# A decode kernel on one core: new row shapes for three weight loads, and a new order of loads and products

## Chip, cores, metric

One core of a Trainium2 chip. The metric is device time in microseconds (us), the median of several executions. The granted TensorE clock is 1.00. A run more than 1.5% above the fastest of its kernel counts as slow. Ratios are the mean time of one kernel's fast runs over the mean of the other's of the same rounds, so they are not quite the ratios of the medians quoted beside them.

## The reference

One token goes through two branches that share its input x (576 numbers) and are mixed by a gate:

```python
g = sigmoid((x * gate_w).sum(-1))
q = (x @ wq)                       # 576 x 4096: 32 query heads of 128
k, v = last 4096 positions of 16 K/V heads (two query heads share one)
a = softmax(q k^T / sqrt(128)) v   # per head
a = a @ wo                         # 4096 x 576
b = gelu(x @ w1 + b1) @ w2 + b2    # 576 x 4608, 4608 x 576
return g * a + (1 - g) * b
```

Everything is bf16. Little is computed and much is read, 53.6 MB in all: K and V are 16 loads of 1 MiB each, wq 4.7 MB, w1, w2 5.3 MB each, wo 4.7 MB.

## The kernel before

All large loads are issued from the SP queue. Most products have one or two moving columns, with the weights as the stationary operand, so that each product on TensorE (PE) needs a weight load of its own (1758 of each in the trace). The first FFN product is the one with w1, the second the one with w2. The parts that matter:

```python
wq_pool = ...tile_pool(name="wq_pool", bufs=3)
for k in range(KT):                      # KT = 5: four tiles of 128 rows, one of 64
    kp = P if k < KFULL else LASTK       # 128, or 64
    wq_k = wq_pool.tile([P, Hq * Dh], BF16, ...)
    nc.sync.dma_start(out=wq_k[:kp, :], in_=A_wq[k*P : k*P+kp, :])
kv_pool = ...tile_pool(name="kv_pool", bufs=5, ...)     # K and V share five buffers
...                                      # x, gate product, q products
for hh in range(5): k_head(hh)           # load K head, 32 products, two exp
w1_t = w1_pool.tile([P, KT, F], BF16)    # five loads, the last of 64 rows
w2_t = w2_pool.tile([P, NF, D], BF16)
nc.sync.dma_start(out=w2_t[:], in_=B_w2.rearrange("(c p) n -> p c n", p=P))   # 1152 B rows
for c in range(NF):                      # first FFN product, 36 chunks
    for k in range(KT):                  # 128, 128, 128, 128, 64 rows
        matmul(ht_ps[:, c:c+1], lhsT=w1_t[:kp, k, c*P:(c+1)*P], rhs=xt[:kp, k:k+1])
    matmul(ht_ps[:, c:c+1], lhsT=b1_row[0:1, ...], rhs=one11)                 # 1 row
...                                      # gelu on DVE and ACT
for hh in range(5, Hkv): k_head(hh)
for c in range(NF):                      # second FFN product
    for j in range(NJ): matmul(acc[j][:, 0:1], lhsT=w2_t[:, c, ...], rhs=gt[:, c:c+1])
    matmul(row[0:1, 512:576], lhsT=gt[:, c:c+1], rhs=w2_t[:, c, 512:576])
...                                      # load wo; per V head: load, 32 products,
                                         # scale, output projection of the head before
```

The text gives no order across engines: the framework schedules this kernel. In the trace K heads 0 to 4 come first, then both FFN products, and K head 5 only after most of the second one.

The softmax here doesn't subtract the row's maximum and nothing guards it: scores larger than these inputs give would overflow.

## Time and profile before

| | before |
|---|---|
| median of the first three runs | 157.19 us (156.29 to 159.23) |
| median of 15 runs | 157.94 us (156.29 to 160.1); of the 12 fast ones 157.64 |
| span of the profiled run | 154.3 us |
| PE busy | 78.8 us, 51% |
| DMA, mean rate | 349 GB/s |

"Span" is one execution in the profile; the measured time is some 2 us more. The prediction below shows the activity rows, the rates by stretch and the waits. One more reading: the stretch of the trace where the second hole ends. Columns are start, duration, engine, line, operation, count.

```profile
74.03 0.99 PE L158 MATMUL s_ps<-qt,kv_t 128*128 128x2 bf16 x32
75.05 7.96 SPq L152 DMA_DIRECT2D kv_t<-in_A_k_cache_dram  x6
```

K head 5's products end at 75.02, and the issue of the next K loads follows at once: the loads had waited for a buffer.

### The profile page before, as it was taken

The page shows a single profiled execution, that of the slowest core. Times are in us where ns is not written, and L with a number is a line of the kernel's source. Part 1 is how long each engine was busy: PE and PEld are TensorE (multiplying, and loading weights), DVE is VectorE, ACT ScalarE, POOL GpSimd, SP SyncE. Part 2 cuts the span into 40 slices and gives each one's busy share as a digit, 9 for nine tenths or more (in the row PEclk, how much of TensorE's full clock was granted, in tenths as well). Part 3 has the DMA queues.
Part 4 walks back from the last instruction along what each step waited for, and adds up shares of the span by engine and source line. Part 5 has one row for each costly group of instructions (what it writes and reads, how often), then busy time and mean ns, then how long its engine had stood idle before and what let it go on. Part 6 is the DMA issues. An engine that isn't in the chain of part 4 may idle for free.

```text
span 154.3 us, 3784 instructions
## 1 busy us (share of the span) xinstructions
PE 78.8 (51%) x1758; PEld 67.8 (44%) x1758; DVE 9.2 (6%) x48; ACT 9.2 (6%) x67; POOL 2.8 (2%) x10
## 2 busy tenths in 40 slices
PE   0181245230007999399996225100266676767671
PEld 0071234220006988377896224100256565656560
DVE  0040000000000000400000000100000000000002
ACT  3000011210000000000123121100000000000000
POOL 7000000000000000000000000000000000000000
DMA  4979999999999999996289999999999999999910
GB/s 146 430 263 357 280 429 418 408 432 423 344 217 356 356 356 400 416 427 255 55 265 397 414 427 361 356 356 390 414 423 416 416 416 418 414 420 414 408 64 2
DMA packets 14802, 53.87 MB, mean 349 GB/s; under 512 B 817, under 2 KB 9538, under 8 KB 9538
## 3 DMA queue, kind: packets, MB, share of 16 engines
q1 hardware_dynamic: 14658, 53.61, 91.5%
q8 instruction: 14, 0.23, 0.6%
q0 software_dynamic: 128, 0.01, 0.1%
q14 instruction: 2, 0.02, 0.0%
HBM read 53.62 MB, written 0.00 MB: 347 GB/s over the span
## 4 chain that ended last, share of the span: by engine, by line
DMA 67%; PE 26%; DVE 2%; issue 1%; SPq 1%; POOL 0%; ACT 0%; DVEq 0%; POOLq 0%
DMA kv_t<-in_A_v_cache_dram 39%; DMA w_t<-in_B_w_dram 15%; DMA kv_t<-in_A_k_cache_dram 9%; PE ht_ps L189 7%; PE acc L238 5%; DMA gw_row<-in_gate_w_dram 4%; PE s_ps L158 3%; PE row L245 3%; PE o_ps L310 3%; PE ht_ps L196 3%; PE qk_ps L133 1%; DVE junk_row L102 0%; DVE out_row L339 0%; POOL x_row L56 0%; PE g_ps L113 0%
## 5 line engine op out<-in xcount | busy, mean ns | idle before, releaser
L310 PE MATMUL o_ps<-et_all,kv_t 128*128 128x2 bf16 x512 | 16.2, 166 | 21.2 <-DMA kv_t<-in_A_v_cache_dram 21.2
L310 PEld LDWEIGHTS <-kv_t 128*128 128x128 bf16 x512 | 14.9, 104 | 23.3 <-DMA kv_t<-in_A_v_cache_dram 23.3
L158 PE MATMUL s_ps<-qt,kv_t 128*128 128x2 bf16 x512 | 15.6, 165 | 16.5 <-DMA kv_t<-in_A_k_cache_dram 16.5
L158 PEld LDWEIGHTS <-kv_t 128*128 128x128 bf16 x512 | 14.6, 104 | 17.4 <-DMA kv_t<-in_A_k_cache_dram 17.3
L189 PE MATMUL ht_ps<-xt,w_t 128*128 128x1 bf16 (+1 forms) x180 | 14.3, 173 | 13.8 <-DMA w_t<-in_B_w_dram 13.8
L189 PEld LDWEIGHTS <-w_t 128*128 128x128 bf16 (+1 forms) x180 | 10.5, 106 | 15.2 <-DMA w_t<-in_B_w_dram 14.2
L238 PE MATMUL acc<-gt,w_t 128*128 128x1 bf16 x144 | 9.6, 170 | 2.4 <-DVE gt L227 2.4
L287 PE MATMUL acc<-ot,wo_t 128*128 128x1 bf16 x128 | 8.2, 167 | 4.0 <-DVE ot L317 4.0
L287 PEld LDWEIGHTS <-wo_t 128*128 128x128 bf16 x128 | 7.1, 105 | 6.0 <-issue 5.0
L166 ACT ACTIVATE et_all<-s_ps 128x32 bf16<-128x32 f32 x32 | 6.2, 204 | 49.8 <-PE s_ps L158 49.8
L238 PEld LDWEIGHTS <-w_t 128*128 128x128 bf16 x144 | 6.7, 106 | 4.6 <-issue 2.3
L133 PE MATMUL qk_ps<-xt,wq_k 128*128 128x1 bf16 (+1 forms) x160 | 4.9, 165 | 6.0 <-DMA wq_k<-in_A_wq_dram 6.0
L245 PE MATMUL row<-w_t,gt 128*1 128x64 bf16 x36 | 7.7, 213 | 0.0
L133 PEld LDWEIGHTS <-wq_k 128*128 128x128 bf16 (+1 forms) x160 | 4.6, 104 | 6.2 <-DMA wq_k<-in_A_wq_dram 6.1
L294 PE MATMUL row<-wo_t,ot 128*1 128x64 bf16 x32 | 6.8, 213 | 0.0
L196 PE MATMUL ht_ps<-one,b_row 1*128 1x1 bf16 x36 | 6.5, 180 | 0.0
L166 ACT ACTIVATION_READ_ACCUMULATOR et_all<-s_ps 128x1 f32 x32 | 6.0, 198 | 0.0
L317 DVE TENSOR_TENSOR ot<-o_ps,rg 128x2 bf16<-128x2 f32 x16 | 2.5, 159 | 49.0 <-PE o_ps L310 49.0
L89 PE MATMUL xt_ps<-one,x_row 1*128 1x1 bf16 (+1 forms) x5 | 0.4, 175 | 6.6 <-DMA x_row<-in_A_x_dram 6.6
L196 PEld LDWEIGHTS <-b_row 1*128 1x128 bf16 x36 | 3.5, 98 | 0.5
L89 PEld LDWEIGHTS <-x_row 1*128 1x128 bf16 (+1 forms) x5 | 0.3, 108 | 6.6 <-DMA x_row<-in_A_x_dram 6.6
L245 PEld LDWEIGHTS <-gt 128*1 128x1 bf16 x36 | 2.8, 79 | 0.5
(50 smaller groups left out, 18.0 us busy)
## 6 DMA issues: line engine op xcount, KB each, us to landing
kv_t<-in_A_k_cache_dram SPq DMA_DIRECT2D x16, 1024.0 KB, 11.7
kv_t<-in_A_v_cache_dram SPq DMA_DIRECT2D x16, 1024.0 KB, 11.4
w_t<-in_B_w_dram SPq DMA_DIRECT2D x1, 5184.0 KB, 35.7
w_t<-in_B_w_dram SPq DMA_DIRECT2D x4, 1152.0 KB, 21.6
wo_t<-in_A_wo_dram SPq DMA_DIRECT2D x1, 4608.0 KB, 25.5
wq_k<-in_A_wq_dram SPq DMA_DIRECT2D x4, 1024.0 KB, 6.1
w_t<-in_B_w_dram SPq DMA_DIRECT2D x1, 576.0 KB, 23.7
wq_k<-in_A_wq_dram SPq DMA_DIRECT2D x1, 512.0 KB
```

Of the source, the lines that this page charges most:

```text
L89: nc.tensor.matmul(xt_ps[:kp, k : k + 1], lhsT=x_row[0:1, k * P : k * P + kp], rhs=one11[0:1, 0:1], start=True, stop=True,)
L133: nc.tensor.matmul(qk_ps[:, j : j + 1], lhsT=wq_k[:kp, j * Dh : (j + 1) * Dh], rhs=xt[:kp, k : k + 1], start=True, stop=True,)
L158: nc.tensor.matmul(s_ps[:, c, :], lhsT=k_t[:, c, :], rhs=qt[:, 2 * hh : 2 * hh + 2], start=True, stop=True,)
L166: nc.scalar.activation(out=et_all[:, hh, :, hq], in_=s_ps[:, :, hq], func=ACT.Exp, scale=SCALE, accum_out=psums[:, 2 * hh + hq : 2 * hh + ...
L189: nc.tensor.matmul(ht_ps[:, c : c + 1], lhsT=w1_t[:kp, k, c * P : (c + 1) * P], rhs=xt[:kp, k : k + 1], start=(k == 0), stop=False,)
L196: nc.tensor.matmul(ht_ps[:, c : c + 1], lhsT=b1_row[0:1, c * P : (c + 1) * P], rhs=one11[0:1, 0:1], start=False, stop=True,)
L238: nc.tensor.matmul(acc[j][:, 0:1], lhsT=w2_t[:, c, j * P : (j + 1) * P], rhs=gt[:, c : c + 1], start=(c == 0), stop=False,)
L245: nc.tensor.matmul(row[0:1, WO_N:D], lhsT=gt[:, c : c + 1], rhs=w2_t[:, c, WO_N:D], start=(c == 0), stop=False,)
L287: nc.tensor.matmul(acc[j][:, 0:1], lhsT=wo_t[:, hq, j * P : (j + 1) * P], rhs=ot[:, hq : hq + 1], start=False, stop=lastq,)
L294: nc.tensor.matmul(row[0:1, WO_N:D], lhsT=ot[:, hq : hq + 1], rhs=wo_t[:, hq, WO_N:D], start=False, stop=lastq,)
L310: nc.tensor.matmul(o_ps[:, 0:2], lhsT=v_t[:, c, :], rhs=et_all[:, hh, c, :], start=(c == 0), stop=(c == NCH - 1),)
L317: nc.vector.tensor_tensor(out=ot[:, 2 * hh : 2 * hh + 2], in0=o_ps[:, 0:2], in1=rg[:, 2 * hh : 2 * hh + 2], op=ALU.mult,)
```

## The change

The intent: keep the load queue from running dry, and give the loads longer rows on all 128 partitions. The order of PE, SP, DVE and ACT is fixed by hand. The diff, cut to its core:

```diff
+    # x[512:576] spread so that partition 2r+h of column 4+h holds x[512+r]
+    xz = const.tile([1, 2, P], BF16, name="xz")
-        nc.sync.dma_start(out=wq_k[:kp, :], in_=A_wq[k * P : k * P + kp, :])
+        if k < KFULL: ...
+        else:         # 64 rows of 4096 -> 128 partitions of 2048
+            nc.sync.dma_start(out=wq_k[:, 0:QH],
+                in_=A_wq[KFULL * P : D, :].rearrange("r (h c) -> (r h) c", h=2))
+    for k in range(3): wq_load(k)
+    ...four w1 loads, then
+    nc.sync.dma_start(out=w1_t[KFULL][:],
+        in_=B_w1[KFULL * P : D, :].rearrange("r (h c) -> (r h) c", h=2))
+    for k in range(3): qk_mm(k)          # q products of a wq tile, added up in SBUF
     ...gate product (was ahead of the q products on PE)
+    hk_mm(0); wq_load(3); hk_mm(1); wq_load(4)   # first FFN product per w1 tile
-    nc.sync.dma_start(out=w2_t[:], in_=B_w2.rearrange("(c p) n -> p c n", p=P))
+    nc.sync.dma_start(out=w2_t[:].rearrange("p (g c) n -> p g (c n)", c=2),
+        in_=B_w2.rearrange("(g p c) n -> p g (c n)", p=P, c=2))
+    for k in range(2, KT + 1): hk_mm(k)  # w1 columns with step 2: cols(i)
+    qk_mm(3); qk_mm(4)
     ...gelu
+    for hh in range(Hkv):
+        k_head(hh)
+        if hh < 12: ffn2(range(3 * hh, 3 * hh + 3))   # 12 acc products, then 3 row products
```

In `out_proj` too the row products now come after the column products.

## The prediction

> **What bounds the kernel now.** I read the activity rows first. They show whether one resource is full from start to end:
>
> ```profile
> PE   0181245230007999399996225100266676767671
> DMA  4979999999999999996289999999999999999910
> GB/s 146 430 263 357 280 429 418 408 432 423 344 217 356 356 356 400 416 427 255 55 265 397 414 427 361 356 356 390 414 423 416 416 416 418 414 420 414 408 64 2
> ```
>
> The DMA engines are the bound: 9 almost everywhere, while PE is mostly half idle. But the GB/s row is not flat. It dips in slices 2 to 4, sits at 217 in slice 11 although the DMA digit there is 9, stays at 356 in slices 12 to 14 and 24 to 26, and falls to 55 in slice 19, the only place where the DMA digit drops and PE is full. The stretch view (PE, PEld, DVE, ACT, POOL, then clock, DMA share, GB/s) gives sizes:
>
> ```profile
> 10.00:12.00 2.00, 1.85 (x65) 1.71 (x62) 1.07 (x6) 0.00 (x0) 0.00 (x0) 1.00 0.41 82
> 15.00:18.00 3.00, 1.01 (x32) 0.93 (x32) 0.19 (x1) 0.00 (x0) 0.00 (x0) 1.00 0.99 229
> 41.00:46.00 5.00, 0.19 (x1) 0.10 (x1) 0.00 (x0) 0.00 (x0) 0.00 (x0) 1.00 0.99 213
> 46.00:58.00 12.00, 10.77 (x151) 9.70 (x151) 0.00 (x0) 0.00 (x0) 0.00 (x0) 1.00 1.08 355
> 71.00:82.00 11.00, 11.00 (x268) 9.51 (x269) 0.00 (x0) 2.03 (x18) 0.00 (x0) 1.00 0.51 172
> 94.00:106.00 12.00, 1.65 (x34) 1.43 (x34) 0.60 (x2) 0.84 (x8) 0.00 (x0) 1.00 1.08 357
> 112.00:146.00 34.00, 23.49 (x560) 19.51 (x557) 2.23 (x14) 0.00 (x0) 0.00 (x0) 1.00 1.01 418
> ```
>
> Two kinds of loss stand here. With a share near 1 but few GB/s, the transfer's shape is slow: 229 is the last wq tile and 213 the last w1 tile (both 64 rows on 64 partitions), 355 and 357 are w2 and wo (1152 B rows). With a low share nobody feeds the queue: 10 to 12 and 71 to 82. The waits of the issuing queue, and PE's timeline, say why:
>
> ```profile
> SPq L152 <- PE s_ps L158: 19.7, 7, 10.8
> SPq L69 <- PE qk_ps L133: 4.7, 2, 4.3
> ```
> ```profile
> 62.27 0.18 PE L196 MATMUL ht_ps<-one,b_row 1*128 1x1 bf16 x1
> 64.82 0.24 PE L238 MATMUL acc<-gt,w_t 128*128 128x1 bf16 x4 [2.37 <-DVE gt L227]
> 65.00 0.21 PE L245 MATMUL row<-w_t,gt 128*1 128x64 bf16 x1
> ```
>
> PE runs the first FFN product from 47.3 to 62.4, waits for the gelu, runs the second FFN product from 64.8, and reaches K head 5 only at 74.0. The five K/V buffers filled up by about 71.6, and the next K load (L152) could be issued only when head 5 freed one at 75.05. At 10 to 12 us, wq tiles 3 and 4 (L69) wait for buffers that the q products free late: in PE's order those stand behind the gate product, which needs a small load.
>
> **What the Trainium skill says.** (1) "SBUF — State Buffer", section "Door 1: The DMA port swizzle": partitions 0 to 63 reach only 8 of 16 ports, asymptote about 218 GB/s. The trace agrees: 229 and 213. (2) "DMA: Bandwidth & Descriptors", "Why small descriptors are slow": a fixed overhead for each packet and descriptor. The trace agrees in kind: its packet records have medians of 55 ns for 1152 B, 313 for 8192 B and 351 for 9216 B, in a line of about 0.037 ns per byte plus 10 to 13 ns. (3) The same page, "Where 436 GB/s comes from", gives 435 as a fabric ceiling and about 358 as a core's HBM limit; this trace runs at 418 for 34 us on one core, so I use 418. (4) "TensorE: Matmul & The Clock Gate", section on weight-path modes: the fast weight load reads packed or strided columns. The change loads w1 with step 2; nothing in the trace of before shows a step, so this is a risk below.
>
> **The change part by part.**
>
> *Row shapes.* The last wq tile becomes 128 partitions of 4096 B, the last w1 tile 128 of 4608 B, and w2 has 2304 B rows (two hidden units per partition; w1's columns are taken with step 2 to match). Fitting a line through the two measured rates (1152 B at 356 GB/s is 51.8 ns a packet per engine, 8192 B at 418 is 313.6) gives 37.2 ps per byte and 9.0 ns fixed. So, as estimates, 2304 B takes 94.7 ns, or 389 GB/s; 4096 to 4608 B about 405 to 409.
> - wq tail: 15 to 18 us moved 3.0 x 229 = 687 KB, which would take 1.64 us at 418: gain 1.36, less about 0.04 for the shorter rows: 1.3.
> - w1 tail and w2: 41 to 58 us moved 5 x 213 + 12 x 355 = 5325 KB. Of it 590 KB at 409 is 1.44 us and 4735 KB at 389 is 12.17 us, 13.6 in place of 17.0: gain 3.4, and 0.1 for the rest of w2: 3.5.
> - wo keeps 1152 B rows: nothing.
>
> *The hole at 10 to 12.* All w1 loads now stand directly behind wq 0 to 2, in own buffers, so that the queue holds some 20 us of work from the start; wq 3 and 4 come after them, long after their buffers are free. The 164 KB moved there take 0.39 us: gain 1.6.
>
> *The hole at 71 to 82.* K heads no longer stand behind an FFN block. The first product runs tile by tile while w1 streams in, and w2 comes before all K heads. The second product is cut into 12 pieces of three chunks, one after each K head. Each K head costs PE 1.05 us (32 products, 1.01 us busy) and three chunks 3 x 0.34 = 1.02 us (the trace's chunks start 0.34 apart): 2.07 us against 2.5 us for a K load (1.049 MB at 418). PE stays ahead, and grouping the row products should help. The stretch moved 11 x 172 = 1892 KB, 4.53 us at 418: gain 6.5.
>
> *What is added.* PSUM is added into SBUF on DVE per w1 tile instead of accumulating in PSUM: six operations near 0.2 us (the qacc additions took 0.19), beside DMA. A w1 tile arrives each 2.8 us; its 36 products take 1.1 us at the K heads' pace of 27 ns, or 2.5 at the 70 ns of the old loop. Both are hidden: after w1, some 17 us of wq and w2 transfers follow before PE needs the gelu. The last wq and w1 products fall from 68 to 34. At the end, grouping row products after the acc products lets the acc copies start perhaps 0.1 us earlier.
>
> *Sum.* 1.3 + 3.5 + 1.6 + 6.5 + 0.1 = 13.0 us: a span of 141.3.
>
> A second count checks this. The first 3.15 MB are in by about 9.95 us, as before. Then, in the new order: w1 at 2.79 us x 4 = 11.2, its tail 1.4, wq 3 2.5, wq 4 1.3, w2 13.6, K 16 x 2.505 = 40.1, wo 13.25 (4.72 MB at 356), V 40.1. Sum 123.4, so the data are in at 133.4. Before, the same reckoning ends at 147.0, with the last V head starting on PE at 148.66 and the span ending 5.64 later: 133.4 + 1.6 + 5.6 = 140.6. The measured time stood 2.0 above the span in the profiled run and 2.9 in the median. So 140.6 + 2.0 = 142.6 is the low reading, 157.2 - 13.0 = 144.2 the high one; I choose 143.4.
>
> **The rivals.**
> 1. *A new wait takes the hole's place.* The program order of the SP queue is now fixed, so one late buffer holds up everything behind it: wq 3 waits for q product 0, K head 5 for head 0 and, through it, for w2 and the gelu. For it: before, this same kind of wait cost 6.5 us. Against it: w2 stands in front of K head 0 in the same queue, so PE has what it needs when K0 lands, and four K loads (10 us) are queued by then. The trace also shows an issue waiting for the load eight places earlier (w2 is issued at 26.01, when K head 2 lands, K head 5 at 29.38 when K head 3 does); eight loads of 1 MB are 20 us of queue, so this does not bind. If it bound, some 5 us would come back: 148.
> 2. *PE becomes the bound.* If step 2 doubles the weight load (55 instead of 27 ns), a w1 tile costs 2.0 us, still under 2.8. If a K head with three chunks passed 2.5 us, 12 heads would lose the excess: at 3.0 us, 6 us, so 149. The trace's 2.07 speaks against it.
> 3. *The transfers do not gain from their shape.* If w2's rows stay at 356, 1.3 us are lost; if the split tails stay at half rate, 2.7: 145 to 147. The port fit in the trace (half the partitions, about half the rate) speaks against the second.
> 4. *Better than reckoned.* Holes between tiles that I did not count close too, and the reading by spans holds: 141.
>
> **Range and chances.** The large terms (the two holes, 8.1 us) rest on measured idle time in a resource that bounds the whole run, and the order of the new queue leaves 10 us of slack. The smaller terms rest on a fit. Range 141.0 to 147.0. Two per cent is 3.1 us; all of the gains but a quarter would have to fail. Faster 0.96, same 0.03, slower 0.01.
>
> **What would show it.** Right: DMA share near 1 without a break from 3 us to the last V load; no 200 to 230 GB/s stretch; w2's stretch near 390 and wo's still near 356; K head 0 starts near 40 us and the last V head near 135; PE shows about 2 us or less of work per K head and waits for K data in each. Wrong: issue waits on s_ps of several us in the K stage, w2 still at 356, PE with no idle between K heads, or a low DMA share near the start of the K stage or at the change to wo.

## The result, and the profile after

The changed kernel takes 143.72 us (143.6 to 143.9, 12 runs) against 157.94 (156.29 to 160.1, 15 runs), or 157.64 for the 12 fast ones: a ratio of 0.9118 of the fast runs, interval 0.9089 to 0.9148. Forecast: 143.4, in 141.0 to 147.0.

The activity rows after, in 40 slices of the span of 142.1 us:

```profile
PE   0164254710004475665745250004537566465661
DMA  4999999999999999999999999999999999999600
GB/s 127 424 424 420 422 415 424 389 391 388 392 417 427 420 420 420 410 420 420 413 422 404 395 356 357 355 404 422 424 404 424 420 417 424 404 427 413 279 25 3
```

The DMA digit is 9 from the second slice to the last V load. No slice before the end of the loads is at 217 or 55 any more. Four slices near 390 are w2 (355 before) and three near 356 are wo, which the change left as it was. By stretch (PE, PEld, DVE, ACT, POOL, clock, DMA share, GB/s):

```profile
10.00:12.00 2.00, 0.77 (x28) 0.77 (x29) 0.18 (x1) 0.00 (x0) 0.00 (x0) 1.00 1.04 440
27.00:39.00 12.00, 1.60 (x48) 1.44 (x48) 2.04 (x10) 0.23 (x1) 0.00 (x0) 1.00 1.05 389
82.00:92.00 10.00, 1.98 (x39) 1.69 (x39) 0.60 (x2) 0.47 (x4) 0.00 (x0) 1.00 1.08 356
```

In the K stage PE is early at every load. The timeline shows one K head with its three chunks of the second FFN product, and the next head's wait; the waits of the SP queue show what is left of its longest wait of before:

```profile
44.68 1.01 PE L267 MATMUL s_ps<-qt,kv_t 128*128 128x2 bf16 x32 [15.64 <-DMA kv_t<-in_A_k_cache_dram]
45.56 0.46 PE L287 MATMUL acc<-gt,w_t 128*128 128x1 bf16 x12
45.94 0.32 PE L295 MATMUL row<-w_t,gt 128*1 128x64 bf16 x3
47.17 1.02 PE L267 MATMUL s_ps<-qt,kv_t 128*128 128x2 bf16 x32 [0.91 <-DMA kv_t<-in_A_k_cache_dram]
```
```profile
SPq L261 <- PE s_ps L267: 11.4, 11, 1.0
```

A head and its chunks take about 1.6 us of 2.5. The eleven waits for a K buffer are now 1.0 us at the longest (10.8 before); they are the ordinary 1.0 us in which PE works on the head that just landed, with four more loads behind it.

### The profile page after: what moved, and what is told of

Same layout as the page of the kernel before. It is cut to its first block, busy times and chain, and to the rows that moved or that the text cites.

```text
span 142.1 us, 3731 instructions
## 1 busy us (share of the span) xinstructions
PE 61.4 (43%) x1725; PEld 53.3 (37%) x1725; DVE 10.5 (7%) x55; ACT 9.1 (6%) x67; POOL 2.8 (2%) x10
## 4 chain that ended last, share of the span: by engine, by line
DMA 90%; PE 6%; SPq 1%; DVE 1%; issue 1%
DMA kv_t<-in_A_v_cache_dram 42%; DMA kv_t<-in_A_k_cache_dram 39%; DMA w<-in_B_w_dram 8%; PE o_ps L368 3%; PE s_ps L267 2%; SPq L93 1%; DVE out_row L397 1%; PE row L389 0%; PE acc L343 0%; PE row L352 0%; DVE ot L375 0%
## 5 line engine op out<-in xcount | busy, mean ns | idle before, releaser
L343 PEld LDWEIGHTS <-wo_t 128*128 128x128 bf16 x128 | 5.9, 104 | 5.0 <-issue 5.0
L343 PE MATMUL acc<-ot,wo_t 128*128 128x1 bf16 x128 | 5.6, 165 | 4.0 <-DVE ot L375 4.0
L159 PE MATMUL hk_ps<-xt,w 128*128 128x1 bf16 x144 | 4.5, 166 | 6.0 <-DMA w<-in_B_w_dram 6.0
L159 PEld LDWEIGHTS <-w 128*128 128x128 bf16 x144 | 4.2, 104 | 6.4 <-DMA w<-in_B_w_dram 6.4
L287 PE MATMUL acc<-gt,w_t 128*128 128x1 bf16 x144 | 5.5, 165 | 0.0
L133 PE MATMUL qk_ps<-xt,wq_k 128*128 128x1 bf16 x128 | 4.0, 166 | 2.8 <-DMA wq_k<-in_A_wq_dram 2.6
L133 PEld LDWEIGHTS <-wq_k 128*128 128x128 bf16 x128 | 3.8, 104 | 3.0 <-DMA wq_k<-in_A_wq_dram 2.8
L287 PEld LDWEIGHTS <-w_t 128*128 128x128 bf16 x144 | 4.8, 104 | 0.0
L352 PE MATMUL row<-wo_t,ot 128*1 128x64 bf16 x32 | 4.3, 226 | 0.0
L295 PE MATMUL row<-w_t,gt 128*1 128x64 bf16 x36 | 3.8, 231 | 0.0
```

The costliest lines, as they stand in the source:

```text
L133: nc.tensor.matmul(qk_ps[:, j : j + 1], lhsT=wq_k[:, j * Dh : (j + 1) * Dh], rhs=xt[:, k : k + 1], start=True, stop=True,)
L159: nc.tensor.matmul(hk_ps[:, i : i + 1], lhsT=w1_t[k][:, cols(i)], rhs=xt[:, k : k + 1], start=True, stop=True,)
L287: nc.tensor.matmul(acc[j][:, 0:1], lhsT=w2_t[:, c, j * P : (j + 1) * P], rhs=gt[:, c : c + 1], start=(c == 0), stop=False,)
L295: nc.tensor.matmul(row[0:1, WO_N:D], lhsT=gt[:, c : c + 1], rhs=w2_t[:, c, WO_N:D], start=(c == 0), stop=False,)
L343: nc.tensor.matmul(acc[j][:, 0:1], lhsT=wo_t[:, hq, j * P : (j + 1) * P], rhs=ot[:, hq : hq + 1], start=False, stop=(last and j2 == 1),)
L352: nc.tensor.matmul(row[0:1, WO_N:D], lhsT=ot[:, hq : hq + 1], rhs=wo_t[:, hq, WO_N:D], start=False, stop=(last and j2 == 1),)
```

## The experiments

Twelve kernels were run, in four sets; all gave correct results. Ten undo or do a part of the change, two (e8, e10) go beyond it. The change itself was not run again beside them; its 12 runs spread over 0.3 us, so the differences to 143.72 are read across sets.

| run | median of the fast runs (from to), us | ratio to before |
|---|---|---|
| after | 143.72 (143.60 to 143.90) | 0.912 |
| e1 order without shapes | 150.57 (149.48 to 150.78; one slow, 152.50) | 0.953 |
| e2 w2 rows back | 145.06 (145.00 to 145.12) | 0.920 |
| e3 both tails back | 148.68 (148.08 to 149.67; one slow, 150.93) | 0.944 |
| e4 shapes without order | 148.94 (148.77 to 149.02) | 0.945 |
| e5 short block | 143.82 (143.73 to 143.91) | 0.912 |
| e6 long block | 148.12 (148.04 to 148.20) | 0.940 |
| e7 old start | 145.61 (145.41 to 145.89) | 0.924 |
| e8 rows of 6912 B | 142.99 (142.84 to 143.16) | 0.909 |
| e9 before, padded rows | 154.03 (153.30 to 154.77) | 0.979 |
| e10 beyond the change | 142.43 (142.31 to 142.51) | 0.905 |
| e11 K heads first | 143.76 (143.61 to 143.85) | 0.914 |
| e12 w1 tail back | 147.54 (146.65 to 147.79) | 0.933 |

### Set 1: shapes against order

**e1**, the change with old shapes (the edits of e2 and e3 together):

> The change with its new order but with the old row shapes (w2 in 1152 B rows, wq and w1 tails on 64 partitions). My theory (the transfers bound the run without a break, so each slow shape costs its full time): the changed kernel's 143.7 plus 1.3 for w2 and about 3.3 for the two tails, so 148.3, and near 356 GB/s for w2 in the profile. Rival (shapes are hidden behind something else and only the order pays): within 1 us of 143.7.

Measured: 150.57. The order alone saves 7.0 us on the median of 157.56 of that set, and the shapes are worth 6.9 on top of it, not 4.6. The rival is out, but my size is too small.

**e2**, w2 back to 1152 B rows:

```diff
-        return slice(g * 2 * P + c, (g + 1) * 2 * P, 2)
+        return slice(i * P, (i + 1) * P)
-        in_=B_w2.rearrange("(g p c) n -> p g (c n)", p=P, c=2),
+        in_=B_w2.rearrange("(c p) n -> p c n", p=P),
```

> The change with w2 back in 1152 B rows and w1 columns without a step. My theory: plus 1.3 us, 145.0, w2 at 356 GB/s, and the w1 weight loads at the same 29 to 31 ns pace as with step 2. Rival A (rows do not matter, 2304 B is no faster): 143.7. Rival B (step 2 slows the weight loads and that is paid somewhere): the first FFN products get faster and the time falls.

Measured: 145.06, plus 1.34. The w2 stretch and a w1 tile's products in e2:

```profile
27.00:39.00 12.00, 1.60 (x48) 1.43 (x48) 2.04 (x10) 0.23 (x1) 0.00 (x0) 1.00 1.09 357
```
```profile
20.62 1.12 PE L158 MATMUL hk_ps<-xt,w 128*128 128x1 bf16 x36 [1.68 <-DMA w<-in_B_w_dram]
```

357 in place of 389 GB/s. 36 products without a step take 1.12 us, and the changed kernel's with step 2 take 1.12 too (shown under e12). The row-length term is right to 0.1 us and a step of 2 costs nothing.

**e3**, both tails back on 64 partitions:

```diff
-                out=wq_k[:, 0:QH],  in_=A_wq[KFULL*P : D, :].rearrange("r (h c) -> (r h) c", h=2)
+                out=wq_k[:LASTK, :], in_=A_wq[KFULL*P : D, :]
-        out=w1_t[KFULL][:], in_=B_w1[KFULL*P : D, :].rearrange("r (h c) -> (r h) c", h=2)
+        out=w1_t[KFULL][:LASTK, :], in_=B_w1[KFULL*P : D, :]
```

> The change with the wq and w1 tails back on 64 partitions. My theory: the wq tail costs about 1.2 us more and the w1 tail about 1.4 to 2.1 us more, so 146.3 to 147.0, with stretches of some 215 to 230 GB/s at about 22 to 29 us. Rival (half of the engines go on with the next tile meanwhile, so that little is lost): under 1 us, 144.5 or less.

Measured: 148.68, plus 5.0 (4.1 by the span of the profiled run, 146.2, which was the fastest of the four). The slow stretches are there, at 206 and 214 GB/s:

```profile
22.00:24.00 2.00, 0.00 (x0) 0.00 (x0) 0.00 (x0) 0.00 (x0) 0.00 (x0) 1.00 1.01 206
27.00:30.00 3.00, 2.16 (x72) 2.07 (x72) 0.39 (x2) 0.00 (x0) 0.00 (x0) 1.00 0.99 214
```

So the tails cost half as much again as the 3.3 that I had, and the fast runs now spread over 1.6 us. e12 follows this up.

**e4**, the kernel before with the new shapes only (split tails, xz, w2 in pairs, w1 columns with step 2; each chunk still accumulates five products and the bias in PSUM):

> The kernel before with only the new row shapes. If the gains simply add, it saves 4.8 us: ratio to before 0.970. My theory after the fact says less: the hole at 71 to 82 us is set by when PE begins the FFN block, which the faster tails bring forward by about 3.3 us, while the 1.3 to 1.5 us from w2's rows only make the hole longer: saves 3.3 us, ratio 0.979, w2 at 390 GB/s and a hole longer than before.

Measured: 148.94 against 157.56, a saving of 8.6. Both figures were far off. The two chunks of the first FFN product, before and in e4, show one reason:

```profile
47.45 0.38 PE L189 MATMUL ht_ps<-xt,w_t 128*128 128x1 bf16 x5
47.77 0.18 PE L196 MATMUL ht_ps<-one,b_row 1*128 1x1 bf16 x1
47.88 0.38 PE L189 MATMUL ht_ps<-xt,w_t 128*128 128x1 bf16 x5
```
```profile
42.73 0.19 PE L209 MATMUL ht_ps<-xt,w_tail 128*128 128x1 bf16 x1 [1.26 <-DMA w_tail<-in_B_w_dram]
42.96 0.27 PE L209 MATMUL ht_ps<-xt,w_t 128*128 128x1 bf16 x4
43.30 0.27 PE L209 MATMUL ht_ps<-xt,w_t 128*128 128x1 bf16 x4
```

The line of five takes in the 64-row product. From one chunk to the next it is 0.43 us before (47.45 to 47.88) and 0.34 in e4 (42.96 to 43.30), with as many products. In e4 none has 64 rows. Over 36 chunks that is 3.1 us of the PE block that makes the hole. The other reason is the start of the block: the w1 tail is in at 42.73, and at 47.22 before, 4.5 us where I had said 3.3. Together 7.6; K head 5 starts at 66.50 in place of 74.03, 7.5 earlier.

### Set 2: the hole, the start, the padding

**e9** tests that PE reason alone: the kernel before with the same loads, but 128-row products of the last w1 tile, upper half zero.

```diff
+    nc.vector.memset(w1_t[LASTK:P, KFULL, :], 0.0)      # and xt zeroed first
-                lhsT=w1_t[:kp, k, c*P:(c+1)*P], rhs=xt[:kp, k:k+1],
+                lhsT=w1_t[:, k, c*P:(c+1)*P],   rhs=xt[:, k:k+1],
```

> The kernel before with its transfers unchanged, but the last w1 tile's products done on 128 rows, the upper 64 being zeros. Made to split the surprise of the shapes-only run, which saved 8.6 us instead of 3.3: there a chunk of the first FFN product takes 0.34 us instead of 0.427. If the switch between 128-row and 64-row products costs PE that 0.087 us per chunk, this kernel saves 36 x 0.087 = 3.1 us of the block that makes the hole: 154.5, ratio 0.980. If the whole surprise came from the transfers, the time stays at 157.6.

Measured: 154.03 against 157.76, 3.7 less; in the profiled runs 151.3 against 154.3, 3.0 less. The ratio of 0.979 (interval 0.974 to 0.983) is clear of 1. Two chunks of it:

```profile
47.27 0.29 PE L190 MATMUL ht_ps<-xt,w_t 128*128 128x1 bf16 x5
47.61 0.29 PE L190 MATMUL ht_ps<-xt,w_t 128*128 128x1 bf16 x5
```

0.34 again, with zeros being multiplied. It is the mixing that costs, not the 64 rows: in e12 below, 36 products of 64 rows in one run take 1.12 us, as 36 of 128 rows do. Mixing 64-row products into a run of 128-row ones costs PE, and in this kernel it cost the whole run, as PE's block held up the loads.

**e5 and e6** put the second FFN product in one block ahead of all K heads, short or long:

```diff
-    for hh in range(Hkv):
-        k_head(hh)
-        if hh < 12: ffn2(range(3 * hh, 3 * hh + 3))
+    ffn2(range(NF))                         # e5: 144 column products, then 36 row products
+    for c in range(NF): ffn2([c])           # e6 instead: 4 column products, 1 row product, ...
+    for hh in range(Hkv): k_head(hh)
```

> The changed kernel with the whole second FFN product (144 column products, then 36 row products) in one block ahead of all K heads, some 6 us on PE once w2 has landed. Theory of buffer slack (a PE block costs the DMA nothing as long as it is shorter than the four or five K loads that are queued, about 10 us less the latency): K head 0 starts near 48.5 instead of 44.7, the next load is issued just in time, and the time is 143.7 to 144.5. Rival (it is the interleaving that closed the hole): several us more, 147 or above.

> As the short block, but in the loop order of the kernel before (four column products, then one row product, per chunk: 0.34 us each in the old trace, 12.2 us in all). Theory of buffer slack: K head 0 starts near 54.5 us, its buffer is free at 55.4, while the five K loads have drained at about 53; with 2 us to first data the queue is dry for some 4 to 4.5 us: 148. Rival (blocks do not matter once w2 stands ahead of K): 143.7 to 144.5.

Measured: e5 143.82, e6 148.12. The block in e5, then K head 0 and the issue of the next K loads in e6:

```profile
42.01 4.00 PE L287 MATMUL acc<-gt,w_t 128*128 128x1 bf16 x144 [12.97 <-DMA w_t<-in_B_w_dram]
45.94 2.08 PE L295 MATMUL row<-w_t,gt 128*1 128x64 bf16 x36
```
```profile
54.33 4.42 PE L267 MATMUL s_ps<-qt,kv_t 128*128 128x2 bf16 x160
```
```profile
55.37 3.74 SPq L261 DMA_DIRECT2D kv_t<-in_A_k_cache_dram  x5
```
```profile
53.00:58.00 5.00, 5.00 (x158) 4.68 (x158) 0.00 (x0) 1.46 (x13) 0.00 (x0) 1.00 0.29 98
```

The same 180 products take 6.0 us grouped and some 12 ungrouped. A block of 6 us costs nothing; one of 12 frees the first buffer at 55.37 (expected 55.4), the queue is dry around it (98 GB/s from 53 to 58), and the run is 4.4 us longer. So interleaving is not needed once the products are grouped. The block has to be shorter than the queued loads last, and grouping alone does that. No run interleaves ungrouped products, so whether the twelve pieces alone would have closed the hole, as the prediction had it, was not tested.

**e11** asks whether the K loads had to move: five K heads go back ahead of w1 tiles 1 to 4 and w2, with the short block.

```diff
-    # all K heads after w2
+    for hh in range(5): k_head(hh)          # after wq and w1 tile 0
+    ...w1 tiles 1 to 4, w2, first FFN product per tile, ffn2(range(NF))
+    for hh in range(5, Hkv): k_head(hh)
```

> The changed kernel with five K heads ahead of w1 tiles 1 to 4 and w2, as the kernel before had them, but with the products per w1 tile and the short second FFN block (6 us). Theory of buffer slack: where the K loads stand in the queue does not matter, only how long PE is kept from freeing buffers; the block delays K head 5 by 3 to 4 us, less than the queued loads last: 143.7 to 144.5. Rival (the new place of the K loads, all after w2, is what removed the hole): a dry stretch after w2, 146 or more.

Measured: 143.76. With the short block, the place of the K loads is indifferent too.

**e7**, the old start:

```diff
-    wq 0, 1, 2, w1 0 to 4, then wq 3, 4;  q products 0 to 2, then the gate product
+    wq 0, 1, 2, 3, 4, then w1 0 to 4;     the gate product, then q products 0 to 2
```

> The changed kernel with the old start: gate product ahead of the q products on PE, wq 3 and 4 ahead of w1 in the queue, waiting for their buffers. My theory: the hole at 10 to 12 us comes back and costs its full 1.3 to 1.7 us: 145.0 to 145.4. Rival (it is made up for later, as engines that are out of step come back into step in a hole): under 0.7 us.

Measured: 145.61, plus 1.89, with the hole back at its old place:

```profile
10.00:12.00 2.00, 1.88 (x70) 1.79 (x67) 0.65 (x3) 0.00 (x0) 0.00 (x0) 1.00 0.40 70
```

70 GB/s against 440. This dry stretch costs its full length, a little over what I had (1.3 to 1.7).

### Set 3: beyond the change

**e8**, six hidden units per partition:

```diff
-        g, c = divmod(i, 2);  return slice(g * 2 * P + c, (g + 1) * 2 * P, 2)
+        g, c = divmod(i, 6);  return slice(g * 6 * P + c, (g + 1) * 6 * P, 6)
-        in_=B_w2.rearrange("(g p c) n -> p g (c n)", p=P, c=2)
+        in_=B_w2.rearrange("(g p c) n -> p g (c n)", p=P, c=6)
```

> The changed kernel with six hidden units per partition instead of two: w2 in 6912 B rows, w1 columns taken with step 6. My theory: by the fitted line a 6912 B row takes 266 ns, 416 GB/s, so w2 takes 12.8 us instead of 13.6: 142.9, and the w1 products keep their 31 ns pace. Rival (the wider step slows the weight loads): the pace doubles, but as PE waits for each w1 tile anyway the time would not show it; only the pace tells. If rows over 2304 B gain nothing: 143.7.

Measured: 142.99, minus 0.73. w2's stretch, and the products of a w1 tile:

```profile
27.00:39.00 12.00, 2.15 (x65) 2.05 (x63) 2.23 (x11) 0.23 (x1) 0.00 (x0) 1.00 1.01 413
```
```profile
20.50 1.84 PE L159 MATMUL hk_ps<-xt,w 128*128 128x1 bf16 x36 [1.94 <-DMA w<-in_B_w_dram]
```

413 GB/s, and 36 products now take 1.84 us in place of 1.12: a step of 12 bytes slows the weight loads (mean record 144 ns against 104), one of 4 bytes does not. PE waits for each w1 tile, so it costs nothing here.

**e10**, e8 with a split last V load and a split last cast:

```diff
+            nc.sync.dma_start(out=v_t[:, 0:24, :], ...)   # last V head only
+            nc.sync.dma_start(out=v_t[:, 24:32, :], ...)
-    nc.vector.tensor_copy(out=out_row[:], in_=row[0:1, 0:D])
+    nc.scalar.copy(out=out_row[:, 0:256], in_=row[0:1, 0:256])
+    nc.vector.tensor_copy(out=out_row[:, 256:D], in_=row[0:1, 256:D])
```

> The 6912 B rows, and two cuts in the chain after the last load: the last V head comes in two loads, so that only 8 of its 32 products wait for the last bytes (24 x 27 ns = 0.64 us less), and the last cast of 576 elements on one partition (0.75 us) is split between ACT and DVE (about 0.35 us less). If the end of the run is the serial chain from the last landing, as the profile has it: 142.9 - 0.9 = 142.0. If the last landing only moves (a second load adds its own latency): 142.9 or more.

Measured: 142.43, the fastest here, but 0.56 below e8 where I expected 0.9. The last casts in its trace:

```profile
137.64 0.36 ACT L399 CAST out_row<-row 1x256 bf16<-1x256 f32 x1 [54.84 <-PE row L391]
138.04 0.48 DVE L400 CAST out_row<-row 1x320 bf16<-1x320 f32 x1 [0.87 <-ACT out_row L399]
```

DVE waits for ACT, as both write one tile, so the cast takes 0.36 + 0.48 one after the other: that part gained nothing against 0.75. The split load gave what there is.

### Set 4: the term that was too small

**e12**, only the w1 tail back on 64 partitions (e3's second edit):

> The changed kernel with only the w1 tail back on 64 partitions, the wq tail left on 128. Made because both tails together cost 4.1 us in the profiled run and 5.5 in the mean, not the 3.3 that I had for them. By bytes alone, 590 KB at 213 GB/s in place of 409 costs 1.3 us: 145.0. With the later start of everything behind it as I read it in the trace of before, 2.0: 145.7. If each tail costs in proportion what the two together did, 2.2 to 2.9: 145.9 to 146.6, and the run-to-run spread (2.9 us with both, 0.3 without) is partly here.

(The 5.5 and the 2.9 in this text take in the slow run of e3; the fast ones give 5.0 and 1.6.)

Measured: 147.54, plus 3.8, more than all three figures. The first FFN products of tiles 3 and 4, in e12 and in the changed kernel:

```profile
26.45 1.12 PE L164 MATMUL hk_ps<-xt,w 128*128 128x1 bf16 x36 [4.80 <-DMA w<-in_B_w_dram]
28.92 1.12 PE L170 MATMUL hk_ps<-xt,w 64*128 64x1 bf16 x36 [1.35 <-DMA w<-in_B_w_dram]
```
```profile
23.25 1.12 PE L159 MATMUL hk_ps<-xt,w 128*128 128x1 bf16 x36 [1.67 <-DMA w<-in_B_w_dram]
24.69 0.64 PE L165 MATMUL hk_ps<-xt,w 128*128 128x2 bf16 x18 [0.32 <-DMA w<-in_B_w_dram]
```

The half-partition load delays the full tile in front of it: tile 3 is used 3.2 us later, the tail itself 4.2, and K head 0 starts at 48.43 instead of 44.68, 3.75 later. Only 1.3 of it is the tail's own bytes at half rate. Where the rest goes can be read in part. Six us around the tail, in e12 and in the changed kernel:

```profile
22.00:28.00 6.00, 1.12 (x36) 1.04 (x36) 0.19 (x1) 0.00 (x0) 0.00 (x0) 1.00 0.95 268
```
```profile
22.00:28.00 6.00, 3.60 (x120) 3.43 (x121) 0.58 (x3) 0.00 (x0) 0.00 (x0) 1.00 1.02 407
```

The DMA share stays near 1, so the engines are for the most part slow rather than idle. They move 834 KB less, which is 2.0 us at 418 GB/s. The packet records of e12 hold 84 slow ones around the tail: 57 of 9216 B (median 0.81 us, usually 0.35) and 27 of the wq tile behind the tail (0.70, usually 0.31); so the slow shape also slows a neighbour. The other 1.7 us of the 3.75 is not in the bytes of this stretch. At the end of the run the rate falls off over 4 us in the changed kernel (360, 246, 147 and 90 GB/s from 132 to 136), and over 6 in e12 (369, 246, 197, 107, 25 and 16 from 134 to 140). That fits my reading that some DMA engines fall behind the others at the tail and stay behind; but these traces do not name the engine of a packet, so it is not shown. What is shown is that in this kernel a slow shape in the middle of a full queue costs about three times what its own bytes at half rate account for. Tails also bring the spread: over fast runs alone, every kernel with a 64-partition load spread over 1.1 us or more, every kernel without one over 0.5 or less.

## Why the prediction was right, point by point

**Bound by the loads: right.** DMA share is 9 tenths or more up to the last V load, and each slow transfer or dry stretch put back shows in the time (e2, e3, e6, e7, e12).

**Row shape of w2: right.** 1.34 measured for 1.3, by the rates 357 and 389 that were forecast as 356 and 389. The fitted line held further out too (413 at 6912 B, 416 forecast).

**Hole at 10 to 12: right.** 1.89 measured (e7) for 1.6.

**Hole at 71 to 82: gone, but what was credited was not needed.** The prediction credited the new place of the K loads and the interleaving. e5 undoes the second and e11 both, at no cost (143.82 and 143.76). What counts is how long PE keeps the first buffer, and grouping the row products, which the prediction named only as a help, is enough (12 us to 6, e6 against e5). That the first product per w1 tile as it arrives counts too is argued: no run undoes it alone. Chunk costs were forecast as 1.02 us for three; grouped, they take about 0.7 (45.56 to 46.26). With a hole of 4.4 us on show in e6, the mechanism (a dry queue behind a long block) is right and the weight of the means was misjudged.

**The w1 tail: the mis-sized term.** The sum had 1.3 for wq's tail and about 2.2 for w1's (3.5 with w2's 1.3). Measured by undoing: 5.0 for both and 3.8 for w1's alone, which leaves about 1.2 for wq's, as forecast, though it was not run by itself. The prediction's own line had a hint: the stretch at 213 GB/s lasts 5 us and moves 1065 KB, and the tail has only 590 KB, so it slowed other bytes as well. Two effects were missing: the neighbours are held up (e12), and in the old loop the 64-row products also slowed PE by 0.09 us a chunk, 3.0 to 3.7 us of the old time (e9).

**Why the total held all the same.** The parts overlap: order alone saves 7.0 and shapes alone 8.6, yet together 13.9 (fast runs), as both shorten the same hole. I read the losses from one trace of before as bytes not moved, which counts each microsecond once whatever its cause. That is bookkeeping, not an experiment: the hole's 6.5 already held what the late tail and the slow chunks had put into it. The second count, by landings, ended 1.5 us early (140.6 against a span of 142.1): K head 0 at 44.68 against 42.5 + 1.6 = 44.1, and the V stage 38.9 us against 37.6. Nearly all of the latter is one step of the V heads of 3.78 us where 2.5 is usual:

```profile
102.73 1.01 PE L368 MATMUL o_ps<-et_all,kv_t 128*128 128x2 bf16 x32 [0.68 <-DMA kv_t<-in_A_v_cache_dram]
106.51 1.02 PE L368 MATMUL o_ps<-et_all,kv_t 128*128 128x2 bf16 x32 [1.98 <-DMA kv_t<-in_A_v_cache_dram]
```

A 16 KB instruction fetch fell into that stretch, but others fell elsewhere without such a step. It is no accident of one run: each of the eleven traces with the new order has one step of 3.0 to 4.0 us among its V heads (e6 at the last), and the three with the old order (before, e4, e9) have none above 2.63. Its cause stays open. The gap between span and time, 1.8 us, is smaller than the 2.0 to 2.9 used (the 2.9 set a median of three runs against the span of another, faster run), which made up for part. So the closeness of 143.4 is partly luck: both span counts were low (141.3 and 140.6 for 142.1), and what was added to them was too much.

**The rivals.** None came about: no issue wait over 1.0 us on the K products, PE at 1.6 of 2.5 us per head, w2 at the rate forecast, and tails that gained more than forecast. **The signs.** All held but one: K head 0 was said to start "near 40 us"; 44.7 is what the second count gives when its landing lag is added, and the sentence left that out.

## What to carry to other kernels

When loads bound a kernel, ask of each block of other work only whether it is shorter than the loads already queued last. If it is, its place did not matter here; if not, shorten it before moving loads about: here grouping products of one shape halved it. Put a short last tile on all 128 partitions. Left on 64, it cost the queue more than its own bytes, its 64-row products slowed a run of 128-row ones when mixed into it, and the time varied from run to run.

## What the Trainium skill lacked or had wrong

- "SBUF — State Buffer", section "Door 1: The DMA port swizzle": the half rate of 64 partitions is right (206 to 229 GB/s here). It does not say that such a load in a full queue delays the full tile ahead of it: 3.8 us for 0.59 MB, where half rate alone is 1.3 (e12), and a run-to-run spread of 1.1 to 2.3 us in fast runs against 0.5 or less.
- "DMA: Bandwidth & Descriptors", "Specifications": it gives 512 B or more as enough for line rate. Here 1152 B rows run at 356, 2304 B at 389, 6912 B at 413 and 8192 B at 418 GB/s (e2, after, e8).
- "SBUF — State Buffer", the note on cachelines, lets bf16 stride by 8 elements for free, and "TensorE: Matmul & The Clock Gate" treats packed and strided fast weight loads alike. Here step 2 is free (1.12 us for 36 products, as without a step), but step 6 takes 1.84 (e8).
- "TensorEngine Tiling (Array Packing)", section "Key Properties", says that a change of the tiling mode drains TensorE, but no page that I read gives the cost of mixing product shapes: 64-row products among 128-row ones add 0.09 us per chunk (e9), and one 64-column row product after every four column products makes 180 products take 12 us instead of 6.0 (e6 and e5).
